# First chunk of a fused attention, gated feed-forward and PReLU feed-forward kernel: where the weight-narrowing steps are issued, and which w_out products are plain float32

## The chip, the cores and the metric

One core of a Trainium2 chip. The metric is the device time of one execution in microseconds. Before the change it is 1598.16 us (median of three runs, 1597.54 to 1599.58). The execution that the profiler recorded took 1597.45 us, of which the profile's span is 1595.7 us.

## The reference

Three layers in a row, in float32 on the outside (some inputs arrive as 64-bit floats and are narrowed on the chip):

```python
# attention through 32 packed queries, batch 8, 8 heads, 576 tokens, head size 64
p_packed = sm_attn(p, k, v)
attn     = sm_attn(q, p_packed, p_packed)
x = attn.transpose(0, 2, 1, 3).reshape(4608, 512)
# gated layer, d_ff 1536
xn = x / sqrt(mean(x*x) + 1e-6) * rms_g
y  = (silu(xn @ w_gate) * (xn @ w_val)) @ w_out
# PReLU layer, d_ff 2048
h  = y @ w_in
out = (max(h, 0) + alpha * min(h, 0)) @ w_out2
```

## The kernel before

The 4608 tokens of the first two layers are worked in twelve **chunks** (512 tokens in the first). Within a chunk the gated layer runs over twelve **column tiles** f = 0 to 11 of 128 columns of d_ff. The order of the instructions on each engine is the order in which the Python code issues them (a manual schedule); each engine works through its own queue in that order.

One column tile f, in the order of issue (the loop over f near L1040 to L1100):

- `blk_in(f, 0, "g")` and `blk_in(f, 256, "v")`: TensorE computes the gate and the value block, twelve passes of 512 columns in all (L122 to L124).
- ScalarE takes the silu (L1071), then **place 1**, `work(f, 1)`; VectorE multiplies silu and value (L1078).
- In a split tile `hsplit` makes the rounded high part hh on ScalarE (L110), then VectorE makes `in_l` (the low part of this tile's w_out, when it is still owed) and `hl` (L113). Then **place 2**, `work(f, 2)`.
- `burst(f, 2)`: in tiles 1, 3, 5, 7, 9 the **job** `wg_job(0, j)`, j = (f + 1) / 2, in tile 11 the first job of the next batch; then pieces of the attention chains (L420 to L698).
- **Place 3**, `work(f, 3)`; `blk_out(f - 1)`, the products of tile f - 1 with w_out into four banks; `burst(f, 3)`; **place 4**, `work(f, 4)`; `both(("o", f + 1))`, which splits the next tile's w_out where it is needed in two parts.

A **job** j multiplies the packed values of the batch with four narrowed weight tiles of w_gate and w_val (L735, 16 passes, four for each weight tile, in their order), and splits the result into `wgh` and `wgl`. Tiles 2j and 2j + 1 read that result in `blk_in`.

**Split and plain products.** In the first chunk `blk_out` of an even tile multiplies plain float32 operands (L1037, two passes for each of four products, eight in all). Odd tiles use high and low parts (L122 to L124, twelve passes).

**Narrowing.** w_gate, w_val and w_out come as 64-bit floats. There are 36 **units** in the first chunk: for each j = 0 to 5 the four weight tiles 6j to 6j + 3 of job j, then the w_out tiles 6j + 4 and 6j + 5. `conv_all` takes the units in pairs and issues one step at a time: first steps of both units of the pair, then second steps of both. A first step is a shift on VectorE (L227) and a conversion on ScalarE (L231). A second step is a combination on VectorE (L233) and an addition on GpSimd (L236), which makes the unit's result. So pair m (units 2m, 2m + 1) has the steps 4m + 1 to 4m + 4, and the second step of the fourth weight tile of job j is step 12j + 8. `n_conv` counts a unit as finished only with the first step of the next pair. `conv(n)` issues n steps. `conv_to(n)` issues steps until n units are finished.

Before the change the code ahead of the chunk issues 13 steps (twelve by `conv(2)` calls, one by `conv_to(5)`). Each tile issues two steps at each of places 1, 2 and 3. At the head of each tile `conv_to` forces what the tile will need: in tile 1 this is six steps; in every other tile none are left to force. So 31 steps are issued by the end of tile 1 and 12j + 13 before tile 2j - 1 begins (j = 2 to 5); the last one is issued in tile 8.

The raw units are loaded by SyncE's DMA queue into eight (from unit 18 on, four) staging buffers; a load waits for the addition that empties its buffer.

Of the kernel before, what the change touches and what calls it, by code (L numbers as in the profile page):

```python
# [18 lines left out]
def attention_moe_moe2_kernel(ctx, tc, q, k, v, p, w_gate, w_val, w_out, rms_g, w_in2, w_out2, alpha, out):  # L19
# [8 lines left out]
    NF = FF // 128  # L28
# [97 lines left out]
    with tc.manual_schedule():  # L126
# [65 lines left out]
        NU1 = len(units)  # L192
# [45 lines left out]
        def conv_unit(n):  # L238
            if n == NU1 // 2:
                sg_ctx.close()  # L240
                late_pools["wg2"] = ctx.enter_context(tc.tile_pool(name="wg2", bufs=NWG - NWG1, reuse_waits="tile"))
            u = units[n]
            w = new_gv() if u[0] == "gv" else wa.tile([128, 4, 128], F32, tag="w", name="w_raw")
            yield from narrow(staged.pop(n), w)
            raw[u] = w
            if u[0] == "gv":
                stores.append((u[1], w))
            while stores and (len(stores) > 3 or n >= NU1 - 2):
                i, w = stores.pop(0)
                nc.sync.dma_start(out=gv_dram[i], in_=w.rearrange("p c x -> p (c x)"))  # L250
            yield

        def conv_late():
# [55 lines left out]
                products((5, b22), (3, b21))  # L309
            yield  # L310

        n_load, n_conv, n_job = [0], [0], [0]

        def loads_to(n):
            while n_load[0] < min(n, NU1):
# [28 lines left out]
        def conv(n):  # L344
            for _ in range(n):
                next(convs, None)

        def conv_to(n):
            while n_conv[0] < min(n, NU1):
                next(convs)  # L350

        in_s = {}

        steady, KEPT = [0], 1
        have, NRO = set(), {"h": 2, "l": 3}

        lo_later = []
# [367 lines left out]
        def wg_job(b, j):  # L725
            if b >= B:
                return
            need_k(b)
            n_job[0] += 1
            ts = [bank("wg") for _ in range(G)]  # L730
            us = [raw.pop(("gv", j * 4 + dc)).rearrange("p c x -> p (c x)") for dc in range(HG)]
            for c_ in range(HG):
                for e in range(2):
                    g, h = c_ // 2, c_ % 2 * 2 + (e ^ c_ // 2)
                    nc.tensor.matmul(  # L735
                        out=ts[g][h * NP:(h + 1) * NP, :],
                        lhsT=ppG[b][e * D:(e + 1) * D, c_, :],
                        rhs=us[c_][e * D:(e + 1) * D, :],
                        start=True, stop=True,
                        tile_position=(e * D, h * NP),  # L740
                    )
            for g in range(G):
                pool = wg1 if n_wg[0] % NWG < NWG1 else late_pools["wg2"]
                n_wg[0] += 1
                h_ = pool.tile([128, 512], F32R, tag="wgh", name="wgh")
                l_ = pool.tile([128, 512], F32R, tag="wgl", name="wgl")
                split_hi(h_, ts[g])
                split_lo(l_, ts[g], h_)
                wgt[b, j, g] = (h_, l_)
            m = b * NJ + j  # L750
            for x in (m + 1, m + 2) if m == NJ - 1 else (m + 2,) if m >= NJ else ():
                gv_load(x)
# [184 lines left out]
        for c, (t0, n, cuts) in enumerate(CH):  # L937
# [9 lines left out]
            def work(f, at):  # L947
                live = [ch for ch in chains["k"] if ch.kind is not None][:1] + chains["q"]
                swap = c > 0 or at == 3 and any(ch.kind == X or ch.kind == M for ch in live)
                if swap and c == 0:  # L950
                    preload(ACTF.Exp)
                for ch in live:
                    n_ = 0
                    while n_ < 2:
                        if ch.kind == R and (at == 1 or at > 2 and (ch is first[0] or n_ == 0)):
                            pass
                        elif n_ == 0 and ch.kind == E and (c == 0 or at < 4) or swap and ch.kind == M:
                            pass
                        elif ch.kind == X and swap and (c == 0 or at == 1 and n_ == 0 or f == NF - 1):
                            pass  # L960
                        else:
                            break
                        ch.last = (c, f, at)
                        ch.next()
                        n_ += 1
                if swap and c == 0:
                    preload(ACTF.Silu)
                if c == 0:
                    conv(2 if at < 4 else 0)

            def q_turn(now, free):
                for n_, ch in enumerate(chains["q"]):
# [21 lines left out]
            def burst(f, at):  # L994
                first[0] = None
                if at == 3 and c and any(ch.kind == X for ch in chains["k"]):
                    return
                jobs = JOBS[c].get(f, ()) if at == 2 else ()
                for jb in jobs if c == 0 else ():
                    wg_job(*jb)  # L1000
                now = [(c, f, x) for x in ((1, 2)[c == 0:] if at == 2 else (2, 3) if c else ())]
                free = 0 if jobs and c else 2
                need = any(ch.b not in ppG for ch in chains["q"])
                if need and (at == 2 or f % 2 == 0):
                    q_turn(now, k_turn(now, free))
                else:
                    k_turn(now, q_turn(now, free))
# [23 lines left out]
                return t  # L1031

            def blk_out(f):
                if c == 0 and f % 2 == 0:
                    h, w = hs.pop(f), raw["o", f]
                    for d in range(KD):
                        nc.tensor.matmul(out=ybk[d], lhsT=w[:, d, :], rhs=h, start=f == 0, stop=f == NF - 1)  # L1037
                    return
                oh, ol = in_s.pop(("o", f))
                hh, hl = hs.pop(f)  # L1040
                for d in range(KD):
                    mm3(ybk[d], oh[:, d, :], ol[:, d, :], hh, hl, f == 0, f == NF - 1)

            for f in range(NF):
                if c == 0 and f == 1:
                    held, hold[0] = hold[0], None
                    for i in held:
                        load_q(i)
                if c == NP1 - 2 and f == 9:
                    y_rows.append(load_rows(0, 0))  # L1050
                if c == 6 and f == 6:
                    nc.sync.dma_start(out=alpha_sb, in_=alpha.rearrange("(f p) -> p f", p=128))
                if c == 0:
                    j1 = (f + 1) // 2
                    conv_to(min(6 * j1 + (5 if f % 2 else 6), NU1))
                if last:
                    if f == 0:
                        assert next(late, late) is late
                        prepare = prep(0)
                    if f > 0:  # L1060
                        next(prepare, None)
                    if f in (2, 4, 6, 8, 10):
                        next(prepare, None)
                    if f > 2:
                        load_next()
                tg = blk_in(f, 0, "g")
                s = ring.tile([128, T], F32, tag="s", name="s")[:, 0:n]
                if c:
                    nc.scalar.activation(out=s, in_=tg, func=ACTF.Tanh, scale=0.5)  # L1069
                else:  # L1070
                    nc.scalar.activation(out=s, in_=tg, func=ACTF.Silu)  # L1071
                work(f, 1)
                if c:
                    nc.vector.scalar_tensor_tensor(  # L1074
                        out=s, in0=s, scalar=1.0, in1=tg, op0=ALU.add, op1=ALU.mult
                    )
                tv = blk_in(f, 256, "v")
                nc.vector.tensor_tensor(out=s, in0=s, in1=tv, op=ALU.mult)  # L1078
                for jb in JOBS[c].get(f, ()) if c else ():
                    wg_job(*jb)  # L1080
                exact = c == 0 and f % 2 == 0
                hs[f] = s if exact else hsplit(s, n)
                if c and 0 < f < NF - 2:
                    work(f, 2)
                if not exact:
                    split_lo(hs[f][1], s, hs[f][0])
                if not (c and 0 < f < NF - 2):
                    work(f, 2)
                burst(f, 2)
                work(f, 3)  # L1090
                late_step(c, f, True)
                if 0 < f < NF - 1:
                    blk_out(f - 1)
                if f < NF - 1:
                    burst(f, 3)
                    work(f, 4)
                if f < NF - 1 and (c or f % 2 == 0):
                    both(("o", f + 1))
                late_step(c, f, False)
            tail = [NF - 2, NF - 1]  # L1100
# [309 lines left out]
```

## Time and profile before

| | before |
|---|---|
| median of three runs | 1598.16 us |
| profiled execution | 1597.45 us |
| span of its profile | 1595.7 us |
| mean granted clock of TensorE | 0.995 |
| first chunk in the trace (first `blk_in` to the last pass of `blk_out`) | 44.5 to 152.6 us |

The profile gives busy time by engine, the chain of work that ended last (followed back from the last instruction: each piece is what released the next), who waited for whom, and instructions in order of time. Times in its rows are from the span's start. A granted clock of 1.00 is full speed (2.4 GHz), 0.50 is half of it (1.2 GHz). A fp32 product is two passes in the trace; "x16" counts passes.

### The profile page before, as it was taken

To read this page: it belongs to the slowest core of one execution; us is meant where nothing else is said; L and a number is where in the kernel's file an instruction comes from. 1 tells how busy PE (TensorE), PEld (TensorE's weight loads), DVE (VectorE), ACT (ScalarE), POOL (GpSimd) and SP (SyncE) were. 2 spreads that over 40 slices of the span, in tenths; PEclk is the share of its full clock that TensorE was granted. 3 is DMA by queue.
4 is the path that set the end of the run, shared out by engine and by line. 5 is a ranking of instruction groups with operands and counts; after the bars stand their busy time and mean duration, and the time that the engine had idled before them with its cause. 6 is when DMAs were issued, how large, how long until landed. Compare 5 with 4: busy or idle time off the path is not lost.

```text
span 1595.7 us, 31864 instructions
## 1 busy us (share of the span) xinstructions
PE 1555.4 (97%) x11762; PEld 1364.9 (86%) x11762; DVE 1161.2 (73%) x2232; ACT 887.8 (56%) x1894; POOL 175.7 (11%) x178
## 2 busy tenths in 40 slices
PE   7799999999999999999999999999999999999999
PEld 5457888887878888889889889988998899999998
DVE  6985766666666666766667778777877787788785
ACT  4666555655556554655555556555655555565564
POOL 1541330111201111211120000000000000000000
PEclk8999999999999999999999999999999999999999
DMA  9886777756677566775555676867676767788776
GB/s 267 275 277 200 232 255 223 220 176 224 225 227 252 161 204 213 261 255 169 205 179 180 192 217 184 250 201 217 185 248 201 211 184 250 260 264 291 259 242 198
DMA packets 239067, 356.29 MB, mean 223 GB/s; under 512 B 63424, under 2 KB 97216, under 8 KB 238912
## 3 DMA queue, kind: packets, MB, share of 16 engines
q1 hardware_dynamic: 238912, 354.25, 70.8%
q8 instruction: 94, 1.54, 0.4%
q14 instruction: 61, 0.50, 0.1%
HBM read 296.50 MB, written 57.67 MB: 222 GB/s over the span
## 4 chain that ended last, share of the span: by engine, by line
PE 82%; DVE 8%; ACT 5%; DMA 2%; issue 1%; SPq 1%; POOL 0%; DVEq 0%; ACTq 0%; POOLq 0%
PE ps_g L122 13%; PE ps_g L123 12%; PE ps_g L124 12%; PE ps_y L122 9%; PE ps_y L123 9%; PE ps_y L124 9%; PE ps_wg L735 3%; PE ps_v L122 3%; PE ps_v L123 2%; PE ps_v L124 2%; PE ps_y L1037 1%; DVE hl L113 1%; ACT hh L110 1%; DVE wgl L113 1%; PE ps_at L658 1%
## 5 line engine op out<-in xcount | busy, mean ns | idle before, releaser
L122 PE MATMUL ps_g<-yh,w 128*128 128x512 f32 (+1 forms) x560 | 206.8, 369 | 2.2 <-DVE tmp L1154 2.2
L123 PE MATMUL ps_g<-yl,w 128*128 128x512 f32 (+1 forms) x560 | 206.3, 368 | 0.0
L124 PE MATMUL ps_g<-yh,w 128*128 128x512 f32 (+1 forms) x560 | 205.7, 367 | 0.0
L122 PE MATMUL ps_y<-hh,in_h 128*128 128x320 f32 (+1 forms) x552 | 195.0, 353 | 0.2
L123 PE MATMUL ps_y<-hl,in_h 128*128 128x320 f32 (+1 forms) x552 | 185.4, 336 | 2.5 <-DVE hl L113 2.4
L124 PE MATMUL ps_y<-hh,in_l 128*128 128x320 f32 (+1 forms) x552 | 184.4, 334 | 0.0
L110 ACT ACTIVATE hh<-kept 128x512 fp32r<-128x512 f32 (+1 forms) x200 | 116.5, 587 | 104.7 <-PE ps_g L123 57.6
L124 PE MATMUL ps_y<-w,hl 128*128 128x256 f32 x576 | 163.4, 284 | 1.5 <-DVE hl L113 1.2
L123 PE MATMUL ps_y<-w,hh 128*128 128x256 f32 x576 | 162.8, 283 | 0.0
L122 PE MATMUL ps_y<-w,hh 128*128 128x256 f32 x576 | 162.5, 282 | 0.0
L110 ACT ACTIVATE hh<-s 128x320 fp32r<-128x320 f32 (+1 forms) x138 | 71.9, 521 | 143.6 <-DVE s L1078 143.4
L122 PEld LDWEIGHTS ps_y<-hh,in_h 128*128 128x128 f32 x552 | 103.6, 188 | 47.5 <-issue 39.2
L113 DVE TENSOR_TENSOR hl<-kept,hh 128x512 fp32r<-128x512 f32 (+1 forms) x200 | 123.3, 632 | 16.2 <-ACT hh L110 15.3
L124 PE MATMUL ps_g<-w,hl 128*128 128x256 f32 x432 | 122.3, 283 | 0.0
L123 PE MATMUL ps_g<-w,hh 128*128 128x256 f32 x432 | 122.3, 283 | 0.0
L122 PE MATMUL ps_g<-w,hh 128*128 128x256 f32 x432 | 122.2, 283 | 0.0
L1154 DVE TENSOR_TENSOR tmp<-tmp,ps_g 128x512 f32<-128x512 f32 (+2 forms) x140 | 88.4, 631 | 45.8 <-PE ps_g L124 45.8
L122 PEld LDWEIGHTS ps_g<-yh,w 128*128 128x128 f32 x560 | 105.4, 188 | 15.5 <-DVE tmp L1154 3.7
L122 PE MATMUL ps_g<-xh,wgh 128*128 128x256 f32 (+3 forms) x352 | 114.1, 324 | 2.7 <-ACT qT L602 1.9
L124 PEld LDWEIGHTS ps_g<-yh,w 128*128 128x128 f32 x560 | 105.1, 188 | 13.5
L123 PEld LDWEIGHTS ps_g<-yl,w 128*128 128x128 f32 x560 | 105.5, 188 | 11.3
L1074 DVE SCALAR_TENSOR_TENSOR s<-s,ps_g 128x320 f32<-128x320 f32 (+1 forms) x132 | 70.6, 535 | 59.4 <-ACT s L1069 58.6
(199 smaller groups left out, 4078.5 us busy)
## 6 DMA issues: line engine op xcount, KB each, us to landing
w<-w_dram SPq DMA_DIRECT2D x280, 256.0 KB, 3.0
w<-o_dram SPq DMA_DIRECT2D x280, 256.0 KB, 3.0
gv_raw<-gv_dram SPq DMA_DIRECT2D x168, 256.0 KB, 4.2
in_l<-lo_dram SPq DMA_DIRECT2D x119, 256.0 KB, 4.5
w<-in_moe_w_out_dram SPq DMA_DIRECT2D x28, 512.0 KB, 5.1
w_dram<-w7o SPq DMA_DIRECT2D x56, 256.0 KB, 2.5
o_dram<-w7o SPq DMA_DIRECT2D x56, 256.0 KB, 2.8
vt<-in_v_dram SPq DMA_DIRECT2D x16, 576.0 KB, 6.3
```

The lines of the kernel that those rows point to most:

```text
L110: nc.scalar.activation(out=hi, in_=src, func=ACTF.Copy)
L113: nc.vector.tensor_tensor(out=lo, in0=src, in1=hi.bitcast(F32), op=ALU.subtract)
L122: nc.tensor.matmul(out=o, lhsT=lh, rhs=rh, start=first, stop=False, skip_group_check=more)
L123: nc.tensor.matmul(out=o, lhsT=lh, rhs=rl, start=False, stop=False, skip_group_check=more)
L124: nc.tensor.matmul(out=o, lhsT=ll, rhs=rh, start=False, stop=last, skip_group_check=more)
L658: nc.tensor.matmul(out=t4[r][:, (k_ * G + g) * 128:(k_ * G + g + 1) * 128], lhsT=AT[rows, g, k_ * rw:(k_ + 1) * rw], rhs=ppbd[par][rows, g ...
L735: nc.tensor.matmul(out=ts[g][h * NP:(h + 1) * NP, :], lhsT=ppG[b][e * D:(e + 1) * D, c_, :], rhs=us[c_][e * D:(e + 1) * D, :], start=True, ...
L1037: nc.tensor.matmul(out=ybk[d], lhsT=w[:, d, :], rhs=h, start=f == 0, stop=f == NF - 1)
L1074: nc.vector.scalar_tensor_tensor(out=s, in0=s, scalar=1.0, in1=tg, op0=ALU.add, op1=ALU.mult)
L1154: nc.vector.tensor_tensor(out=out, in0=x, in1=y, op=ALU.add)
```

## The change

- A unit is counted as done (`n_done`) when its second step is issued, and `conv_to` counts by that. The step ahead of the chunk that `conv_to(5)` issued falls away.
- Places 1, 2 and 3 issue one, two and three steps in place of two each. The forcing at the head of each tile is taken out; in its place there is one `conv_to` ahead of each job and one ahead of each `both`.
- The tiles with plain products are 0, 2, 4, 6 in place of 0, 2, 4, 6, 8, 10. Tiles 8 and 10 are split.
- In tile 1 `blk_out(0)` is issued ahead of `burst(1, 2)`, that is ahead of job 1, in place of after `work(1, 3)`.

```diff
             while stores and (len(stores) > 3 or n >= NU1 - 2):
                 i, w = stores.pop(0)
                 nc.sync.dma_start(out=gv_dram[i], in_=w.rearrange("p c x -> p (c x)"))
+            n_done[0] += 1
             yield
...
-        n_load, n_conv, n_job = [0], [0], [0]
+        n_load, n_conv, n_job, n_done = [0], [0], [0], [0]
...
         def conv_to(n):
-            while n_conv[0] < min(n, NU1):
+            while n_done[0] < min(n, NU1):
                 next(convs)
...
-        steady, KEPT = [0], 1
+        steady, KEPT, PLAIN = [0], 1, (0, 2, 4, 6)
...
                 if c == 0:
-                    conv(2 if at < 4 else 0)
+                    conv(at % 4)
...
                 for jb in jobs if c == 0 else ():
+                    conv_to(6 * ((f + 1) // 2) + 4)
                     wg_job(*jb)
...
             def blk_out(f):
-                if c == 0 and f % 2 == 0:
+                if c == 0 and f in PLAIN:
...
-                if c == 0:
-                    j1 = (f + 1) // 2
-                    conv_to(min(6 * j1 + (5 if f % 2 else 6), NU1))
...
-                exact = c == 0 and f % 2 == 0
+                exact = c == 0 and f in PLAIN
...
+                ahead = c == 0 and f == 1
+                if ahead:
+                    blk_out(0)
                 burst(f, 2)
                 work(f, 3)
                 late_step(c, f, True)
-                if 0 < f < NF - 1:
+                if 0 < f < NF - 1 and not ahead:
                     blk_out(f - 1)
...
-                if f < NF - 1 and (c or f % 2 == 0):
+                if f < NF - 1 and (c or f + 1 not in PLAIN):
+                    if c == 0:
+                        conv_to(6 * ((f + 1) // 2) + 5 + (f + 1) % 2)
                     both(("o", f + 1))
```

With the change 12 steps are issued ahead of the chunk and six in each of tiles 0 to 9; none of the `conv_to` calls finds anything to force.

## Rows read from the trace of the kernel before

**Rows 1.** The page's head and its line for TensorE: busy time, share of the span, instructions.
```profile
span 1595.7 us, 31864 instructions
PE 1555.4 (97%) x11762; PEld 1364.9 (86%) x11762; DVE 1161.2 (73%) x2232; ACT 887.8 (56%) x1894; POOL 175.7 (11%) x178
```
**Rows 2.** Busy time of each engine by stretch: tiles 0 and 1, then tiles 2 to 11.
```profile
44.50:69.80 25.30, 17.09 (x83) 8.79 (x83) 25.24 (x33) 14.06 (x27) 14.79 (x11) 0.87 0.86 266
69.80:152.60 82.80, 82.03 (x564) 53.80 (x563) 60.90 (x121) 53.97 (x111) 30.86 (x24) 1.00 0.76 241
```
**Rows 3.** The chain that ended last, 40 to 155 us: start, length, what.
```profile
64.25 5.17 PE ps_y L1037 x8
...
69.80 0.43 PE ps_g L122
...
75.29 0.23 PE ps_y L124
...
79.61 1.02 PE ps_wg L735 x16
81.09 3.44 PE ps_y L1037 x8
...
95.14 1.02 PE ps_wg L735 x16
```
**Rows 4.** TensorE in order of time: start, length, passes, idle before and its releaser.
```profile
57.97 0.60 PE L735 MATMUL ps_wg<-gv_raw,ppG 64*32 64x512 f32 x2
63.04 1.21 PE L442 MATMUL ps_at<-kT,pT 64*32 64x288 f32 x14 [4.48 <-DVE s L1078]
...
114.20 0.66 PE L600 MATMUL ps_at<-ident,qt 128*128 128x128 f32 x4 [0.77 <-DVE s L1078]
```
**Rows 5.** VectorE in order of time, tiles 0 and 1.
```profile
49.84 0.67 DVE L1078 TENSOR_TENSOR s<-s,ps_v 128x512 f32<-128x512 f32 x1
...
54.81 2.93 DVE L227 TENSOR_SCALAR w_raw<-w 128x512 int32<-128x512 int32 x2
```
**Rows 6.** GpSimd in order of time: additions of units 8 and 9.
```profile
54.42 3.04 POOL L236 TENSOR_TENSOR gv_raw<-gv_raw,w 128x512 int32<-128x512 int32 x2 [1.02 <-DMA w<-in_moe_w_val_dram]
```
**Rows 7.** Groups of instructions in the first chunk: count, busy us, mean ns, idle before.
```profile
L236 POOL TENSOR_TENSOR gv_raw<-gv_raw,w 128x512 int32<-128x512 int32 x20 | 26.8, 1340 | 26.8 <-DVE gv_raw L233 13.9 <-ACT wgh L110 2.2 <-DMA w<-in_moe_w_out_dram 2.1
L233 DVE SCALAR_TENSOR_TENSOR gv_raw<-w,gv_raw 128x512 int32<-128x512 int32 x20 | 15.2, 766 | 0.0
L227 DVE TENSOR_SCALAR gv_raw<-w 128x512 int32<-128x512 int32 x20 | 15.0, 763 | 1.8 <-DMA w<-in_moe_w_val_dram 1.8
L113 DVE TENSOR_TENSOR in_l<-w_raw,in_h 128x512 fp32r<-128x512 f32 x6 | 6.7, 1113 | 0.0
L113 DVE TENSOR_TENSOR hl<-s,hh 128x512 fp32r<-128x512 f32 x6 | 4.1, 686 | 0.3
```
**Rows 8.** VectorE in order of time, tile 5 and a line of tile 9.
```profile
95.42 0.69 DVE L1078 TENSOR_TENSOR s<-s,ps_v 128x512 f32<-128x512 f32 x1
96.02 1.44 DVE L113 TENSOR_TENSOR in_l<-w_raw,in_h 128x512 fp32r<-128x512 f32 x1
...
98.21 0.64 DVE L233 SCALAR_TENSOR_TENSOR gv_raw<-w,gv_raw 128x512 int32<-128x512 int32 x1
...
130.93 0.70 DVE L647 STREAM_TRANSPOSE A2T<-A 128x512 f32<-128x512 f32 x1
```
**Rows 9.** GpSimd in order of time, the addition behind it in tile 5.
```profile
99.07 1.29 POOL L236 TENSOR_TENSOR gv_raw<-gv_raw,w 128x512 int32<-128x512 int32 x1 [2.17 <-DVE gv_raw L233]
```
**Rows 10.** TensorE by one-microsecond stretch: length, busy (passes), granted clock, DMA share, GB/s.
```profile
33.00:34.00 1.00, 0.00 (x0) 0.59 1.07 246
39.00:40.00 1.00, 1.00 (x12) 0.50 1.03 367
60.00:61.00 1.00, 0.00 (x0) 0.74 1.18 232
66.00:67.00 1.00, 1.00 (x3) 0.50 1.01 385
```

## The prediction

> **What bounds the kernel now.** I read the page's head and engine table first. TensorE is busy 97% of 1595.7 us [rows 1], so time is lost or won only where TensorE stands still or where its work changes. The change touches the first chunk, so I split that by stretch [rows 2]. In tiles 0 and 1 (44.5 to 69.8 us) TensorE is busy 17.09 of 25.30 us at a mean granted clock of 0.87, while VectorE is busy 25.24: VectorE bounds there. In tiles 2 to 11 TensorE is busy 82.03 of 82.80 at full clock: TensorE bounds, and anything that makes it wait is paid in full, here and in the 90% of the span behind it, where nothing waits for the first chunk's end but TensorE itself. Then the chain of waits gives the joints [rows 3], and the engine timelines say why they are where they are: job 1 ends at 58.57, TensorE then idles 4.48 us until VectorE's multiplication of tile 1, which stands behind the forced narrowing steps [rows 4, 5]. In tile 7 there is a second, small wait of 0.77 us for the same reason [rows 4]. The reader is to see that the two long idle stretches before 70 us are the only reserve: 8.2 us of idle, and what the half clock costs there: `blk_out(0)` took 5.17 us where `blk_out(2)` took 3.44 [rows 3].
>
> **What is moved, counted in steps.** Job j needs step 12j + 8, the second step of its fourth weight tile. Before, 12j + 13 steps are issued when tile 2j - 1 begins, so the job's data were made a tile earlier, and job 2 follows `blk_in(3)` at once, 1.02 us long [rows 3]. After, 12 steps stand ahead of the chunk and 6 in each tile. At the head of tile 2j - 1 that is 12j + 6; place 1 issues step 12j + 7, place 2 steps 12j + 8 and 12j + 9. So the last addition of the job is queued on VectorE behind that same tile's multiplication, `in_l` and `hl`, which all need this tile's value block from TensorE. And TensorE has the job next in its queue. Only tile 1 has other work in front of it (`blk_out(0)`). In tiles 3, 5, 7 and 9 TensorE must stand still from about three quarters of the job (12 of 16 passes) until the addition is done.
>
> **Term 1, tiles 0 and 1: -8.0 us.** In tile 0, two of three narrowing instructions in front of the multiplication go; they take some 0.76 us each [rows 7], more when an addition of GpSimd runs beside them (2.93 for two, [rows 5]). I take 1.9 us: the multiplication starts at about 48.0 in place of 49.84 [rows 5], and `blk_in(1)`, which waits for its bank, some 1.7 us earlier, at 49.2. In tile 1 six steps less stand in front of the multiplication. `blk_out(0)` follows `blk_in(1)` at full clock (52.2 to 55.7). Unit 9's addition: from 48.6, the end of tile 0's multiplication, six narrowing instructions (4.6), the multiplication 0.69, `in_l` 1.11, `hl` 0.69, the combination 0.77, 0.2 to GpSimd and 1.34 give 58.0 by the means [rows 7]; with two more shifts drawn out as in [rows 5] 59.2, which I take, as that stretch is the crowded one (before: 57.46, [rows 6]). So job 1 ends near 59.6, against 58.57. Then come the 64 x 288 products (0.7 to 1.2 us, [rows 4]) and the split of the job's result, whose cover `blk_out(0)` has moved away: `blk_in(2)` waits for the banks until about 61.8. Before it starts at 69.80 [rows 3]. Bounds: -10.5 (the 8.2 idle, 1.7 of slow `blk_out(0)` and 0.6 of the slow products) and -3.4 (only `blk_out(0)` hidden). I take the worked value.
>
> **Term 2, four waits: +16.8 us.** From the end of `blk_in` in tile 2j - 1: 0.1 to the multiplication, 0.69 for it, 1.11 `in_l`, 0.69 `hl`, 0.77 the combination, 0.22 to GpSimd, 1.34 the addition, 0.1 back, 0.27 for the job's last four passes: 5.3 us by the means [rows 7], where the job now takes 1.02. That is +4.2 each. The trace has the same row of instructions in tile 5, for a unit that was not urgent: `blk_in(5)` ends at 95.14 [rows 3], the multiplication starts at 95.42, the combination behind `hl` at 98.21 and its addition ends at 100.36 [rows 8, 9]; with 0.1 and 0.27 the job would have ended 5.6 after `blk_in`, +4.6. Without any overlap of `in_l` with an addition it is 0.69 in place of 1.11 to 1.44, so +3.7. Bounds +3.4 and +5.0 each; I take the means.
>
> **Term 3, where VectorE is behind: +2.4 us.** In tile 3 the early gain of 8 us has run into VectorE's backlog (six steps and the attention chain's pieces between two multiplications): +0.7. In tile 9 a transposition of 0.70 stands in front of place 2 [rows 8]: +0.7. Tile 8, now split, gets `in_l` and `hl` on VectorE and one step more than before, so tile 9's multiplication is late by about 1.0. Bounds 0 and 4 together.
>
> **Term 4, the second stall goes: -0.8 us.** Tile 7's multiplication stood behind steps of units that job 5 needs [rows 4]; these now come later.
>
> **Term 5, tiles 8 and 10 split: -1.4 us.** Eight float32 passes take 3.44 us [rows 3], twelve of 0.23 us [rows 3] 2.76: -0.7 each. The extra `hh` on ScalarE and the two subtractions on VectorE (0.69 and 0.69 to 1.11, [rows 7]) lie beside TensorE's next `blk_in`; in tile 10 narrowing is over. The part that isn't covered is in term 3.
>
> **Term 6, the clock: +4.0 us.** TensorE's clock fell to half after such waits: in the idle microsecond 33 to 34 it falls to a mean of 0.59 and is still 0.50 at 39 to 40; in the idle one at 60 it falls to 0.74 and is 0.50 at 66 to 67 [rows 10]. A wait of some 4 us behind `blk_in` is about as long as those. It would then be `blk_out` of the tile before that runs slow at first. Bounds 0 and 1.7 us each (5.17 less 3.44, [rows 3]); I take 1.0, since the wait is shorter than the one at 60.
>
> **At nothing.** SyncE's loads of a pair are issued with the first step of the pair two before, four steps ahead of their use, as now; with longer odd tiles that is more time, so no new wait (if it were, the cost is like the 0.77). Stores of the last job's weight tiles move behind the loads for the next batch, which tile 11 needs 15 us later. GpSimd's additions, moved back, pass the chain's small power step in tile 6; its reader is half a tile later.
>
> **Sum.** -8.0 + 16.8 + 2.4 - 0.8 - 1.4 + 4.0 = +13.0 us. The profiled execution, 1597.45, becomes 1610.5; its distance to the median shown, 0.7, makes it 1611.2; I say 1611.
>
> The rows show `in_l` at 1.44 us when an addition of GpSimd runs beside it, against a mean of 1.11 [rows 7, 8]. The Trainium skill, GPSIMD Engine Reference, section 1 Specifications, says that GpSimd shares its SBUF interfaces with VectorE, with contention for VectorE instructions that have two SBUF inputs. By it every one of the four waits has the longer `in_l`, since place 1 issues an addition right in front of the multiplication; the sum would be 4 x 0.33 = 1.3 us higher.
>
> **The rivals.** (a) Faster: the waits are covered. The mechanism is the freed start: `blk_in(2)` 8 us earlier, and the job's last addition ready when TensorE reaches it. Terms 1, 4 and 5 alone give -10.2, 1588 us. For it speaks VectorE's 100% in tiles 0 and 1, relieved by six steps. Against it: the order of issue lets no addition of step 12j + 8 start before this tile's value block is done. It decides where the four waits cost less than 10.2 us together, 2.6 each. (b) The waits are there, the clock holds: +9.0, 1607. For it: from tile 2 on the clock is 1.00 through every small wait [rows 2]. Against: rows 10. The Trainium skill, TensorE: Matmul & The Clock Gate, section on HAM oscillation, tells of a kernel whose array fell to half rate at every wait between bursts of matmuls; by that rule term 6 stays and this rival falls. (c) VectorE's backlog grows: term 1 is -5, the waits 5.0 each, term 3 is 4 and the clock 1.7 each: +23.6, up to 1621. For it: VectorE's share in tiles 0 and 1; against: 60.90 of 82.80 afterwards [rows 2]. (d) Gain and waits cancel: -10.5 and 3.4 each, no lag, no clock: +0.9, 1599.
>
> **How the numbers follow.** The forecast 0.38, (a) 0.15, (b) 0.24, (c) 0.15, (d) 0.08. A difference under 0.2%, 3.2 us, is about what a measurement of this kernel cannot tell from none. (a) gives faster 0.15, (d) same 0.08, the rest slower 0.77. The slower cases alone lie in 1602 to 1621. The range takes in (d) and the ends of the terms on the good side: 1596 to 1621, which leaves out (a) and the tails.
>
> **What would show it.** In the profile after: the pieces L735 of jobs 2 to 5 in the chain end some 5 us after the last pass of the value block, TensorE's wait there is put down to GpSimd's L236, four times 3 to 4.5 us; `blk_in(2)` starts near 62; the granted clock dips behind the waits; `blk_out(8)` and (10) appear as twelve passes of 0.23 us; the first chunk ends near 165 in place of 152.6. The prediction is wrong if job 2 follows `blk_in(3)` without a wait, or if tile 2 starts at 62 and job 5 no later than before.

## The result, and the profile after

The changed kernel takes 1620.68 us (median, 1617.88 to 1623.11) against 1597.85 us for the one before on the same chip: ratio 1.0143, 95% interval 1.0121 to 1.0165. It is 22.8 us slower; forecast were 13. The profiled executions stand at 1621.71 and 1597.45, 24.3 apart.

The page's head and engine lines of the kernel after, which answer to [rows 1]: TensorE's busy time grew by 11.6 us, the span by 24.2, so a little more than half of the loss is TensorE standing still; the rest is work that took longer.

```profile
span 1619.9 us, 31881 instructions
PE 1567.0 (97%) x11770; PEld 1369.7 (85%) x11770; DVE 1161.5 (72%) x2236; ACT 890.8 (55%) x1898; POOL 176.4 (11%) x178
```

The same two stretches as in [rows 2], tiles 0 and 1, then tiles 2 to 11 (columns: length, busy of TensorE, its weight loads, VectorE, ScalarE, GpSimd, granted clock, DMA share, GB/s):

```profile
46.12:63.72 17.60, 15.14 (x82) 9.26 (x83) 13.99 (x19) 9.83 (x17) 8.80 (x6) 0.90 0.73 203
63.72:175.17 111.45, 94.93 (x568) 58.41 (x569) 71.60 (x139) 61.33 (x125) 37.64 (x28) 0.92 0.61 195
```

Tiles 0 and 1 got 7.6 us shorter. Tiles 2 to 11 got 28.7 longer: TensorE, busy all but 0.8 us there before, now stands still for 16.5, and the granted clock's mean fell from 1.00 to 0.92. The joints by TensorE's timeline (start, length, what, idle before and its releaser): `blk_out(0)`, `blk_in(2)`, the job in tile 3, `blk_out(2)`, the end of the job in tile 5, `blk_out(4)`, the end of the job in tile 7, and the job in tile 9.

```profile
54.73 3.59 PE L1039 MATMUL ps_y<-s,w_raw 128*128 128x512 f32 x8
...
63.72 0.50 PE L122 MATMUL ps_g<-xh,wgh 128*128 128x512 f32 x1 [0.54 <-DVE wgl L113]
...
74.89 1.06 PE L736 MATMUL ps_wg<-gv_raw,ppG 64*32 64x512 f32 x8
76.29 1.05 PE L736 MATMUL ps_wg<-gv_raw,ppG 64*32 64x512 f32 x4 [0.33 <-POOL gv_raw L236]
79.54 1.29 PE L736 MATMUL ps_wg<-gv_raw,ppG 64*32 64x512 f32 x4 [2.20 <-POOL gv_raw L236]
81.42 4.70 PE L1039 MATMUL ps_y<-s,w_raw 128*128 128x512 f32 x8
...
102.02 1.92 PE L736 MATMUL ps_wg<-gv_raw,ppG 64*32 64x512 f32 x4 [2.48 <-POOL gv_raw L236]
105.17 4.77 PE L1039 MATMUL ps_y<-s,w_raw 128*128 128x512 f32 x8
...
126.37 1.05 PE L736 MATMUL ps_wg<-gv_raw,ppG 64*32 64x512 f32 x4 [2.20 <-POOL gv_raw L236]
...
143.30 1.06 PE L736 MATMUL ps_wg<-gv_raw,ppG 64*32 64x512 f32 x8 [0.95 <-DVE kT L119]
147.23 1.05 PE L736 MATMUL ps_wg<-gv_raw,ppG 64*32 64x512 f32 x4 [2.87 <-POOL gv_raw L236]
151.08 1.06 PE L736 MATMUL ps_wg<-gv_raw,ppG 64*32 64x512 f32 x2 [2.80 <-POOL gv_raw L236]
```

From the end of `blk_in` to the end of the job are now 5.94 us in tile 3, 7.27 in tile 5, 6.43 in tile 7 and 10.7 in tile 9 (its last two passes end at 152.99): 30.3 where the four took 4.6. That is 25.8 of the 28.7. The three plain `blk_out`s behind the jobs, (2), (4) and (6), took 4.70, 4.77 and 3.60, where the same timeline has 3.60 for each in the kernel before; that is another 2.3. `blk_out(2)` there:

```profile
80.92 3.60 PE L1037 MATMUL ps_y<-s,w_raw 128*128 128x512 f32 x8
```

Only 8 of the 16 passes are ready at once; the next four wait for one addition, the last four for another.

Why, on VectorE and then GpSimd in tile 3: the job's last combination (77.31) stands behind the multiplication, `in_l` and `hl`; its addition ends at 79.49 and the passes start at 79.54.

```profile
72.59 1.53 DVE L227 TENSOR_SCALAR gv_raw<-w 128x512 int32<-128x512 int32 x1
...
75.07 0.69 DVE L1077 TENSOR_TENSOR s<-s,ps_v 128x512 f32<-128x512 f32 x1 [0.35 <-PE ps_v L124]
75.67 1.11 DVE L113 TENSOR_TENSOR in_l<-w_raw,in_h 128x512 fp32r<-128x512 f32 x1
76.71 0.68 DVE L113 TENSOR_TENSOR hl<-s,hh 128x512 fp32r<-128x512 f32 x1
77.31 0.68 DVE L233 SCALAR_TENSOR_TENSOR gv_raw<-w,gv_raw 128x512 int32<-128x512 int32 x1
```
```profile
74.94 1.29 POOL L236 TENSOR_TENSOR gv_raw<-gv_raw,w 128x512 int32<-128x512 int32 x1 [1.11 <-DMA w<-in_moe_w_val_dram]
78.21 1.28 POOL L236 TENSOR_TENSOR gv_raw<-gv_raw,w 128x512 int32<-128x512 int32 x1 [1.97 <-DVE gv_raw L233]
```

In tile 9 VectorE itself is late, behind drawn-out shifts and the chain's pieces (`blk_in` ends at 142.3, the multiplication starts at 145.49):

```profile
139.70 2.98 DVE L227 TENSOR_SCALAR gv_raw<-w 128x512 int32<-128x512 int32 x2
142.60 0.54 DVE L119 COPY kT<-ps_at 128x384 f32<-128x384 f32 x1
...
145.49 0.68 DVE L1077 TENSOR_TENSOR s<-s,ps_v 128x512 f32<-128x512 f32 x1
146.08 1.64 DVE L113 TENSOR_TENSOR in_l<-w_raw,in_h 128x512 fp32r<-128x512 f32 x1
...
148.88 0.64 DVE L233 SCALAR_TENSOR_TENSOR gv_raw<-w,gv_raw 128x512 int32<-128x512 int32 x1
```

The clock at the jobs' ends in tiles 3, 5, 7 and 9 (columns as above, so the granted clock is the third number from the end): 0.56, 0.50, 1.00 and 0.50. Behind tile 7's wait there is no dip.

```profile
80.00:82.00 2.00, 2.00 (x8) 0.98 (x5) 0.51 (x1) 0.93 (x2) 0.00 (x0) 0.56 0.85 324
102.00:106.00 4.00, 3.98 (x11) 1.76 (x12) 1.36 (x5) 1.67 (x4) 0.00 (x0) 0.50 0.87 320
128.00:130.00 2.00, 2.00 (x10) 1.04 (x8) 1.90 (x4) 1.70 (x4) 0.13 (x1) 1.00 0.67 231
150.00:154.00 4.00, 2.92 (x21) 0.73 (x21) 0.79 (x2) 0.94 (x2) 1.02 (x1) 0.50 0.81 297
```

A piece lies outside the first chunk. SyncE's timeline has eight loads for the next batch spread over 26 us, then the last three stores; below it the longest wait of these loads.

```profile
144.28 26.05 SPq L723 DMA_DIRECT2D gv_raw<-gv_dram  x8
170.38 1.37 SPq L250 DMA_DIRECT2D gv_dram<-gv_raw  x3
```
```profile
SPq L723 <- PE ps_wg L736: 17.1, 1, 17.1
```

The sixth load waited 17.1 us for the job of tile 11, which frees its buffer. Such a wait stood in the kernel before too (14.3 us at the longest). New are the three stores behind it: the last four loads wait for them and go out from 171.85 to 176.86. From the end of the first chunk to the store of the second chunk's result it is 77.5 us instead of 75.2. Summed: 1.6 (the chunk starts later), 21.2 (the chunk), 2.3 (the second chunk), together 25.1 at that store, and -0.8 in all that follows: 24.3.

The 1.6 is no part of the change. The start of `blk_in(0)` varies from 44.1 to 47.9 us in all traces here, and the work that runs in front of it is the same in both kernels. I therefore compare tiles by their distance from `blk_in(0)`.

### The profile page after: what moved, and what is told of

Its sections match the earlier page's. It is cut to its first block, busy times and chain, and to the rows that moved or that the text cites. A ratio compares the mean times of both kernels' runs of the same rounds, so it can differ in the third digit from the quotient of the medians.

```text
span 1619.9 us, 31881 instructions
## 1 busy us (share of the span) xinstructions
PE 1567.0 (97%) x11770; PEld 1369.7 (85%) x11770; DVE 1161.5 (72%) x2236; ACT 890.8 (55%) x1898; POOL 176.4 (11%) x178
## 4 chain that ended last, share of the span: by engine, by line
PE 77%; DVE 6%; ACT 4%; DMA 1%; issue 1%; ACTq 0%; DVEq 0%
PE ps_g L122 13%; PE ps_g L123 12%; PE ps_g L124 12%; PE ps_y L122 9%; PE ps_y L123 9%; PE ps_y L124 8%; PE ps_wg L736 3%; PE ps_v L122 2%; PE ps_v L123 2%; PE ps_v L124 2%; DVE hl L113 1%; ACT hh L110 1%; PE ps_at L659 1%; DVE yl L113 1%; DVE wgl L113 1%
## 5 line engine op out<-in xcount | busy, mean ns | idle before, releaser
L123 PE MATMUL ps_y<-hl,in_h 128*128 128x320 f32 (+1 forms) x560 | 188.8, 337 | 2.0 <-DVE hl L113 1.9
L124 PE MATMUL ps_y<-hh,in_l 128*128 128x320 f32 (+1 forms) x560 | 187.7, 335 | 0.0
L123 PEld LDWEIGHTS ps_y<-hl,in_h 128*128 128x128 f32 x560 | 105.5, 188 | 10.4 <-DVE hl L113 4.4
```

The source lines that it names most:

```text
L123: nc.tensor.matmul(out=o, lhsT=lh, rhs=rl, start=False, stop=False, skip_group_check=more)
L124: nc.tensor.matmul(out=o, lhsT=ll, rhs=rh, start=False, stop=last, skip_group_check=more)
```

## The experiments

Unless another base is named, the edits are made in the kernel after. Each ratio is to the kernel before on the same chip; the runs come from several chips, on which that kernel stood at 1597.85 to 1598.66 us. Edits are shown shortened. Names of theories: W, the jobs' waits for their last additions; S, the split of tiles 8 and 10 overloads VectorE; Q, SyncE's queue; L, VectorE or the loads cannot narrow faster.

**The parts alone.** First the moved steps alone, without early `blk_out(0)` and with all even tiles plain:

```
-PLAIN = (0, 2, 4, 6)          +PLAIN = range(0, NF, 2)
-ahead = c == 0 and f == 1     +ahead = False
```

> The changed kernel with only the narrowing part: blk_out(0) back behind job 1, even tiles plain again. W: nearly all of the 23 us stay, plus 1 to 2 for tile 1: about 1622. S (the split tiles make VectorE late in tile 9, where the longest wait is): 4 us or more come back, 1616.

Measured: 1621.77 us, 1.0153 [1.0134, 1.0172]. The steps alone carry a loss as large as the whole change's; S falls. Second, in the kernel before, the two other parts one at a time: the column tiles,

```
-if c == 0 and f % 2 == 0:     +if c == 0 and f in PLAIN:   # (0, 2, 4, 6)
```

(and the same at the two other places that ask for it)

> The kernel before with only the plain tiles changed (0, 2, 4, 6; tiles 8 and 10 split). Theory W (the loss is TensorE's wait for each job's last addition, which the new issue order puts behind the same tile's multiplication and splits): the split alone gains 2 x 0.7 = 1.4 us, about 1596.5. Rival S (the two split tiles overload VectorE and make the following multiplications late): 2 to 4 us slower than before, about 1601. Rival Q (SyncE's queue, blocked for 17 us by loads that wait for stores behind them): no change, 1598.

and `blk_out(0)` ahead of job 1:

```
+ahead = c == 0 and f == 1
+if ahead:
+    blk_out(0)
...
-if 0 < f < NF - 1:
+if 0 < f < NF - 1 and not ahead:
```

> The kernel before with only blk_out(0) moved ahead of job 1 in tile 1. W: blk_out(0) fills part of the hole of 13 us ahead of tile 2 at full clock, but the products of 64 x 288 still wait for tile 1's multiplication and tile 2 for the split of the job's result on VectorE: tile 2 starts near 67.4 in place of 69.8, gain 2 to 5 us, about 1594.5. S and Q: the same, so this run only measures the part.

Measured 0.9999 [0.9991, 1.0008] and 0.9998 [0.9989, 1.0007], both misses, with intervals of 1 to 2 us to either side. The first shows no slowdown either, so S falls here too. In its trace tile 11 does get 0.7 us shorter (from its last value pass to the next chunk 7.2 instead of 7.9), but tile 9 nothing: the products of the chain in front of `blk_out(8)`, 0.94 us before, took 1.41, and tile 10 was 0.5 longer. In the second `blk_out(0)` runs at full clock (3.59 us) and tile 2 starts 22.8 us after `blk_in(0)` in place of 25.2, near what was expected; but the chunk as a whole is only 1.2 us shorter, which the median does not show. TensorE stands idle behind `blk_out(0)`: two waits for VectorE, and a mean clock of 0.68 in the 6 us after them. Its timeline, tile 1:

```profile
66.38 0.71 PE L442 MATMUL ps_at<-kT,pT 64*32 64x288 f32 x14 [4.25 <-DVE s L1078]
...
70.07 0.69 PE L600 MATMUL ps_at<-ident,qt 64*128 64x64 f32 x4 [2.98 <-DVE wgl L113]
```

The wait that `blk_out(0)` was to fill reappeared behind it, since VectorE bounds there.

**The waits (W).** The same six steps a tile, but two at each of places 1, 2 and 3, so that step 12j + 8 is issued at place 1, in front of the multiplication, `in_l` and `hl`:

```
-conv(at % 4)                  +conv(2 if at < 4 else 0)
```

> The changed kernel with two steps at each of places 1, 2, 3 again, nothing else undone: the job's last addition is then issued in place 1, ahead of the tile's multiplication, in place of behind multiplication, in_l and hl. W: the four waits shrink from 6.1, 7.4, 6.6 and 10.9 us to some 2 us each, 20 us come back, about 1601. Q: the stores of the last job's weight tiles still stand behind the loads, so 17 us or more of the 23 stay, about 1618. S: tiles 8 and 10 are still split, 1617 to 1620.

Measured: 1606.02, 1.0048 [1.0036, 1.0061]; 14.7 of the 22.8 are back (15.2 by the ratios), where 20 were expected. The job in tile 3 (4.3 us in place of 5.9) and its wait in tile 9:

```profile
71.59 1.06 PE L736 MATMUL ps_wg<-gv_raw,ppG 64*32 64x512 f32 x8
73.12 1.05 PE L736 MATMUL ps_wg<-gv_raw,ppG 64*32 64x512 f32 x4 [0.47 <-POOL gv_raw L236]
74.82 1.05 PE L736 MATMUL ps_wg<-gv_raw,ppG 64*32 64x512 f32 x4 [0.65 <-POOL gv_raw L236]
...
134.65 2.75 PE L736 MATMUL ps_wg<-gv_raw,ppG 64*32 64x512 f32 x6 [3.01 <-POOL gv_raw L236]
```

The four jobs still last 22.2 us in this trace, against 4.6 before the change. Less the 9.1 us by which tiles 0 and 1 are shorter, that is about the loss that is left.

The other way to take a wait off TensorE is to give it work: `blk_out(f - 1)` ahead of the job in every odd tile.

```
-ahead = c == 0 and f == 1     +ahead = c == 0 and f in (1, 3, 5, 7, 9)
-    blk_out(0)                +    blk_out(f - 1)
```

> The changed kernel with blk_out of the tile before put ahead of the job in tiles 3, 5, 7 and 9 too, as it is in tile 1. W: 2.8 to 3.4 us of work fill each wait and the clock holds, but the split of the job's result loses its cover and blk_in of the next tile waits 1 to 2 us for it: 8 to 12 us come back, about 1611. If the waits were not what is lost (S, Q): no change or slower, 1621 or more.

Measured: 1606.80, 1.0065 [1.0051, 1.0079]; 13.9 back (12.5 by the ratios), more than the 8 to 12 expected. The job in tile 3 is down to 2.3 us, the one in tile 5 to 3.6:

```profile
75.86 1.07 PE L736 MATMUL ps_wg<-gv_raw,ppG 64*32 64x512 f32 x12
77.10 1.05 PE L736 MATMUL ps_wg<-gv_raw,ppG 64*32 64x512 f32 x4 [0.17 <-POOL gv_raw L236]
93.02 1.07 PE L736 MATMUL ps_wg<-gv_raw,ppG 64*32 64x512 f32 x12
95.55 1.05 PE L736 MATMUL ps_wg<-gv_raw,ppG 64*32 64x512 f32 x4 [1.46 <-POOL gv_raw L236]
```

Two edits that share only the waits bring back about the same, so W is shown for some 12 to 15 us. What the clock lost behind the waits is in this sum: the mean granted clock is 0.995 in both profiles, as before the change, and 0.989 in the kernel after. **The queue (Q):** the last stores are issued four units sooner, ahead of the loads.

```
-while stores and (len(stores) > 3 or n >= NU1 - 2):
+while stores and (len(stores) > 3 or n >= NU1 - 6):
```

> The changed kernel with the stores of the last job's four weight tiles issued at once with each tile, so that they stand ahead of the next batch's loads in SyncE's queue. W: the first chunk ends as late as before this edit; only chunk 1, whose keys and queries came late, gains: 0 to 2.5 us, about 1619. Q: the queue is free from 152 to 169 us and 15 us or more come back, about 1605.

Measured: 1618.99, 1.0128 [1.0115, 1.0142]. The second chunk is back at 75.2 us, so the 2.3 were the queue's; the wait of the loads for tile 11's job is still there (13.2 us), but no store stands behind it. It is a small term.

**What a lead costs.** If waits are all, a kernel with the job's steps one tile ahead should win by the 8 us of tiles 0 and 1. First seven steps a tile from tile 2 on:

```
-conv(at % 4)                  +conv(at % 4 if f < 2 else (0, 2, 2, 3)[at % 4])
```

> The changed kernel, from tile 2 on with 2, 2, 3 steps at the places in place of 1, 2, 3: the lead grows by one step a tile, so the last addition of jobs 3, 4 and 5 is issued a tile ahead, that of job 2 in place 1 of its own tile. W (the waits for the last addition are the loss): jobs 3 to 5 follow their value block without a wait, job 2 waits some 2.5 us; the early start of tile 2 (8 us) stays; about 1592. Rival L (VectorE and the loads can't do more than six steps a tile: the waits come back as late multiplications): 1605 or more.

then eight in tile 2 (2, 3, 3) and 2, 2, 2 behind it, with the stores early:

```
-conv(at % 4)
+conv(at % 4 if f < 2 else 0 if at > 3 else (2, 3, 3)[at - 1] if f == 2 else 2)
```

> The changed kernel with 2, 3, 3 steps in tile 2 and 2, 2, 2 from tile 3 on, and the last job's stores issued at once: the last addition of each of jobs 2 to 5 is the last step of the tile before. W: no wait or under 1 us at each job, TensorE bounds from tile 2 on, and the start's gain stays: 1588 to 1592. L: multiplications of tiles 2 and 3 late by 2 us more, 1596.

Measured 1603.26, 1.0033 [1.0020, 1.0045], and 1601.16, 1.0020 [1.0011, 1.0029]: most of the loss is gone, and no gain appears; the second is slower than either theory had it. In the second, tile 2 starts 16.6 us after `blk_in(0)` (before 25.2), tile 4 35.4 (40.2), tile 6 53.9 (57.6), tile 8 71.6 (74.3), tile 10 92.6 (90.5): the early gain is given back tile by tile, most of it in tiles 2 and 3 and in tiles 8 and 9. VectorE's busy time (third of the busy columns) in 65 to 105 us, first this kernel, then the one before:

```profile
65.00:85.00 20.00, 18.79 (x115) 10.98 (x113) 19.06 (x30) 13.74 (x26) 12.47 (x10) 1.00 0.81 278
85.00:105.00 20.00, 19.55 (x180) 12.51 (x178) 19.01 (x39) 11.54 (x26) 10.53 (x8) 1.00 0.88 249
```
```profile
65.00:85.00 20.00, 20.00 (x107) 12.19 (x106) 17.38 (x31) 13.62 (x28) 9.43 (x7) 0.94 0.83 279
85.00:105.00 20.00, 20.00 (x194) 12.85 (x194) 17.93 (x43) 13.63 (x27) 10.47 (x9) 1.00 0.89 286
```

95% against 88%. That the steps which the start no longer carries make VectorE the limit in these tiles (L) is read from these shares; no run here shows it by itself. Three variants of it followed. All even tiles plain:

```
-PLAIN = (0, 2, 4, 6)          +PLAIN = range(0, NF, 2)
```

> As e8 (last additions one tile ahead, early stores, blk_out(0) ahead of job 1), but all even tiles plain as before the change. Theory L (with the waits gone, VectorE, 95% busy from 65 to 105 us in e8, bounds the first chunk, so that the early start is given back tile by tile): without the extra splits of tiles 8 and 10 VectorE has 2.8 us less to do where it is late (tiles 8 and 9), 1.4 us of TensorE time come back in: 1597 to 1599. If TensorE's passes were the bound in tiles 8 to 10 instead: 1.4 us slower than e8, 1602.5.

1603.66, 1.0035 [1.0023, 1.0048]: a miss, 2.5 us more than with tiles 8 and 10 split, and so against L in tiles 8 and 9. In its trace the last two `w_out` shifts wait 1.41 and 1.73 us for their loads, and TensorE 3.19 us in tile 9 for the multiplication behind them. Then, with all even tiles still plain, two steps more in tile 1 and one fewer in tile 2:

```
+conv(0 if at > 3 else ((1, 2, 3), (1, 4, 3), (1, 3, 3), (2, 2, 2))[min(f, 3)][at - 1])
```

> As e9, with two steps more in tile 1, issued ahead of the split of job 1's result where VectorE idled 2.2 us, and one step a place later in tile 2: VectorE's idle time at the start is used and the lead is one step larger. L: job 2's wait of 2.2 us goes and the gain of tile 1 is kept longer: 1594 to 1597. If the loads or GpSimd bound the narrowing rather than the order on VectorE: as e9.

1601.55, 1.0022 [1.0013, 1.0030]; and the same with tile 10 split, `PLAIN = (0, 2, 4, 6, 8)`:

> As e10, with tile 10 alone split (no narrowing is left there). L: blk_out(10) is twelve passes in place of eight float32 ones, 0.7 us less, and VectorE has room: 1593.5 to 1596.5, 0.7 below e10. S: as e10 or slower.

1600.03, 1.0010 [1.0001, 1.0019]. Both miss the gain. In the last one tile 9 lasts from 77.1 to 93.0 us after `blk_in(0)` (before 81.1 to 90.5; the 77.8 to 95.1 in the expectation below are those of the run ahead of it). Its VectorE, SyncE and TensorE timelines:

```profile
129.01 0.43 DVE L227 TENSOR_SCALAR w_raw<-w 128x512 int32<-128x512 int32 x1 [5.42 <-DMA w<-in_moe_w_out_dram]
```
```profile
119.16 4.17 SPq L250 DMA_DIRECT2D gv_dram<-gv_raw  x5
123.43 1.19 SPq L214 DMA_DIRECT2D w<-in_moe_w_out_dram  x2
```
```profile
130.04 2.15 PE L736 MATMUL ps_wg<-gv_raw,ppG 64*32 64x512 f32 x16 [2.74 <-DVE kT L119]
...
134.44 4.79 PE L1039 MATMUL ps_y<-s,w_raw 128*128 128x512 f32 x8
```

The narrowing step waits 5.42 us for its load, and `kT`, the multiplication and so TensorE stand behind it on VectorE. Five stores, which my own edit had put there, stood ahead of that load. The last kernel takes that edit back:

```
-while stores and (len(stores) > 3 or n >= NU1 - 6):
+while stores and (len(stores) > 3 or n >= NU1 - 2):
```

> As e11, but the early issue of the stores is taken back (n >= NU1 - 2), so that no stores stand ahead of the last two w_out loads on SyncE's queue. In e11 five stores waited there from 119.16 to 123.33 us, the two loads were issued at 123.43, and tile 9 then lasted from 77.8 to 95.1 us of the chunk, against 81.1 to 90.5 in before. If those stores delayed the narrowing of tile 9 (theory O, order on the queue): the loads go out about 119 us, tile 9 gets 3 to 4.5 us shorter and the kernel is at 1595.5 to 1597 us, ratio 0.998 to 0.9995. If VectorE's work alone sets these tiles (theory L): tile 9 changes by less than 1 us, and the kernel stays at 1600 us or gets up to 2 us slower, since the loads of the next batch stand behind the last stores again. I expect O at 0.5.

Measured: 1597.23, 0.9995 [0.9986, 1.0004], level with the kernel before. Tile 9 is 1.9 us shorter, not 3 to 4.5: between the two theories.

```profile
129.02 0.43 DVE L227 TENSOR_SCALAR w_raw<-w 128x512 int32<-128x512 int32 x1 [4.45 <-DMA w<-in_moe_w_out_dram]
```
```profile
121.74 1.23 SPq L214 DMA_DIRECT2D w<-in_moe_w_out_dram  x2
```
```profile
130.06 1.27 PE L736 MATMUL ps_wg<-gv_raw,ppG 64*32 64x512 f32 x16 [1.76 <-DVE kT L119]
...
133.97 3.70 PE L1039 MATMUL ps_y<-s,w_raw 128*128 128x512 f32 x8
```

The loads went out 1.7 us sooner (2.2 counted from `blk_in(0)`) and the step still waited 4.45. TensorE's two waits in tile 9 add up to the same, 2.74 and 0.42 us before, 1.76 and 1.47 now. What differs is the clock: 1.00 from 130 to 138, where it had been 0.50 to 0.73, so that `blk_out(8)` took 3.70 instead of 4.79. That the shorter first wait kept the clock up is not shown by itself. No kernel here beats the one before. Whether one would whose last `w_out` loads are issued about 115 us, as in the kernel before, was not tried.

## Why the prediction held in kind and missed in size

The main step was right, and the waits cost more than was forecast: step 12j + 8 is queued behind `in_l` and `hl`, TensorE has the job next, and the wait is put down to GpSimd's L236. That 1620.68 still lies inside the range of 1596 to 1621 is in part luck, since its upper end was rival (c)'s, whose working is not what happened. By terms:

- **Term 1** (-8.0): right, -7.6. `blk_in(2)` starts 17.60 us after `blk_in(0)`, forecast 17.3.
- **Term 2** (+16.8) **and term 3** (+2.4): mis-sized; jobs and lag measured 25.8 against 19.2. Three details failed. "12 of 16 passes" were to be ready; 8 were, as the addition of place 1 was late too. The last four passes were priced at 0.27 us, a quarter of the job; alone they take 1.05 to 1.92. And the lag stood elsewhere: none in tile 3, 3.2 us in tile 9, where I had 0.7 for a transposition and 1.0 for tile 8's split. What stood there, one after the other from 138.16 on, were three shifts, three combinations, `kT`, a reduction, two small steps and a product of the chain; two of those shifts took 2.98 us beside GpSimd's additions. The 1.0 for the split was about right: in the kernel with the steps alone, tile 8 plain, the multiplication is still 1.9 us late and the job lasts 9.3 in place of 10.7. The backlog without the split is what was missing. Tile 9's job alone is 9.6 of the 25.8.
- **Term 4** (-0.8): right; no wait for VectorE's multiplication is left in tile 7.
- **Term 5** (-1.4): half of it is in the traces, the 0.7 of tile 10's split. The kernel with the column tiles alone gains 0.0 (interval -1.4 to +1.3): in its tile 9 the multiplication came 0.8 us after the value block in place of 0.3, and tile 10 was 0.5 longer.
- **Term 6** (+4.0): about right; 2.3 in the plain `blk_out`s, and more inside the jobs, where it is counted above (1.92 for four passes in tile 5). It fell behind three of four waits, in tiles 3, 5 and 9. Rival (b), a clock that holds, falls. The Trainium skill, TensorE: Matmul & The Clock Gate, section on HAM oscillation, tells of a kernel whose array fell to half rate at every wait between bursts of matmuls. Three of the four waits here agree with that, and tile 7's does not.
- **At nothing:** wrong for SyncE. I looked at whether the loads need to be early, not at whether the stores behind them would hold up the loads that come after: +2.3 us.
- **Rivals:** (c), the backlog, gave 1621, near the time measured, but not by its own working: it had term 1 at -5 and 5.0 in each wait. (a) and (d) fall.

In each of the four waits an addition of GpSimd overlapped `in_l`, which took longer than the 0.69 us it takes alone (tile 8): 1.45 and 1.64 us in tiles 7 and 9, 1.11 and 1.10 in tiles 3 and 5, where the addition overlaps only its first half. The price of 1.44 for every wait was met in half the cases. The bigger victim is the shift L227: 0.41 us alone, 1.53 beside an addition. The Trainium skill, GPSIMD Engine Reference, section 1 Specifications, names contention with GpSimd for VectorE instructions that have two SBUF inputs. For `in_l` the trace agrees.

## What to carry to other kernels

When steps are moved from a forced point to their place of use, follow the last step that a consumer needs through every queue that it crosses, with what is queued in front of it at the new place; one place of difference was worth 14.7 us here. Price the tail of a job that waits by a short burst's own row, not by its share of the whole job. And look, before a step is moved forward, at whether its load can come earlier too: in the last kernel the step waited 4.45 us for it. Whether a busy engine alone would have taken the gain away stays open here.

## What the runs showed that I had not expected

- One load that waited for its buffer stopped SyncE's queue for 17 us (152 to 169 us); from 156 to 170 the DMA engines moved 0 GB/s. A stop of 14.3 us stood there before the change too. What cost 2.3 us are the three stores caught behind it.
- A wait of 1.76 us on TensorE left the clock at 1.00, one of 2.74 at the same place (ahead of the job in tile 9) was followed by 0.50, and `blk_out(8)` paid 1.1 us for it. In the kernel after, tile 3's wait of 2.20 was followed by 0.56 and tile 7's of 2.20 by 1.00; in the kernel with the steps alone a wait of 2.21 in tile 7 was followed by 0.58 and one of 2.49 in tile 5 by 1.00. The length of the wait alone does not decide it; what does stays open here.
- The distance of `blk_in(0)` from the start differs by up to 3.8 us between executions of the same work, more than the 0.2% that these comparisons can resolve; single traces are only comparable from there on.
